# Grouping tokens by batch in the loads of an attention, soft mixture-of-experts and softplus kernel

## The chip, the cores and the metric

The kernel runs on one core of one Trainium2 chip. The metric is the device time of one execution in microseconds (us). An execution has five compute engines at its disposal (TensorE for matmuls and transposes, here PE; VectorE, DVE; ScalarE, ACT; GpSimd, POOL; SyncE, SP, which only issues DMAs here) and 16 DMA engines that move data between HBM and the on-chip memory of 128 partitions.

## What is computed

Three stages follow each other. q, k and v have the shape (8 batches, 8 heads, 576 tokens, 64). Attention is inside chunks of 64 tokens; the output is laid out as x with 8 x 576 = 4608 rows (tokens) of 512. A soft mixture of experts mixes all 4608 rows into 32 slots by a softmax over the tokens, runs 8 experts on their slots, and mixes the slots back into each token. A softplus layer ends it.

```python
def _attn_ref(q, k, v):                       # (8, 8, 576, 64) each
    chunk = 64; nc = S // chunk; scale = 1.0 / np.sqrt(D)
    scores = scale * np.matmul(q_c, k_c.transpose(0, 1, 2, 4, 3))   # per chunk
    attn = softmax(scores)
    out = np.matmul(attn, v_c)
x = attn_out.transpose(0, 2, 1, 3).reshape(B * S, H * D)            # (4608, 512)
logits = x @ phi                              # 32 slots
d = softmax of logits over the tokens
slot_out = per expert: relu((d.T @ x) @ w1[e]) @ w2[e]
x = (softmax of logits over the slots) @ slot_out
h = x @ w_in
g = np.maximum(h, 0.0) + np.log1p(np.exp(-np.abs(h)))
out = g @ w_out                               # (4608, 512)
```

## The kernel before

**Groups, pairs, units.** The 4608 tokens are cut into NG = 9 groups of GT = 512 in running order, over the ends of the batches: since a batch has 576 tokens, group 0 is the first 512 tokens of batch 0, group 1 the last 64 of batch 0 and the first 448 of batch 1, and so on, until group 8 is the last 512 tokens of batch 7. Each group has eight heads; a unit is two heads of a group (36 units), a pair is two units, four heads (18 pairs). Loads are by pair, work is by unit.

**Loads.** `load_q` (L297) loads q or k of a pair into a tile of 128 partitions; a partition holds four consecutive tokens of each head, 1 KB a head. `load_v` (L305) loads v in four blocks of 128 tokens, one token a partition, 256 bytes a head. Both ask `runs` (L288) for the stretches that lie in one batch and issue one DMA for each. So groups 0 and 8 load q in one piece of 128 partitions, and the others in two, of 16 and 112, 32 and 96, 48 and 80, 64 and 64, 80 and 48, 96 and 32, 112 and 16 partitions. In odd groups one block of v is split into 64 and 64. All DMAs are issued from SP, in order. q and k have two buffers each, v has three. Every issue also waits for the completion of the eighth DMA before it.

**The front.** For a unit: PE transposes q and k (`st_A`, L428), ACT copies them out (`st_B`, L440), PE makes the scores (`st_S`, L453), DVE subtracts the row maximum (L465, the one instruction of that line per unit, and L471), ACT takes the exponential, PE transposes (L486), PE multiplies with v (L505), DVE divides (L528), PE transposes the result x (L540). After the four units of a group come the logits (L556) and the running sums over tokens (up to `acc`, L624). Beside this, SP loads w_in in 16 pieces of 512 KB (`load_wi`, L340), which DVE, ACT and POOL convert, and some pieces of w1 (`load`, L326 and L329) that are parked until they are used.

**What sets the order.** `issue` is a list planner: it gives every step a rank and a cost by the table COST (SP: 3.4 for a load of q and k, 2.7 for v, 1.35 for w_in), and records the steps engine by engine in the order in which it would start them. The costs are those of the steps, not of the DMAs inside them.

**After the front.** The weights of the experts stream in through slots that are refilled as PE frees them (`emit_H`, `emit_SO`); their order is a list written by hand. The softplus stage then runs over 18 output tiles t of TT = 256 tokens, two per group, each in two halves i of 128 tokens (`emit_oc`, L1149, stores them). Inside a 512-token group, the odd tile has its two 64-token halves swapped over the partitions, so it is stored in two pieces of 64 rows.

Of the kernel before, what the change touches and what calls it, by code (L numbers as in the profile page):

```python
# [183 lines left out]
def kernel(  # L184
# [12 lines left out]
    nc = tc.nc  # L197
    B, H, S, D = q.shape
# [6 lines left out]
    TT = 256  # L205
    GT = 512
# [4 lines left out]
    NG = NT // GT  # L211
# [73 lines left out]
    vb = [ap.tile([128, 4, 4, VW], F32, name=f"vb{i}") for i in range(NV)]  # L285


    def runs(t0, n):  # L288
        done = 0
        while done < n:  # L290
            b, s = divmod(t0 + done, S)
            step = min(n - done, S - s)
            yield done, step, b, s
            done += step


    def load_q(src, t, pr, hs=range(4)):  # L297
        G, h0 = pr // 2, 4 * (pr % 2)
        for off, n, b, s in runs(G * GT, GT):
            nc.sync.dma_start(  # L300
                out=t[off // 4:(off + n) // 4, hs[0]:hs[-1] + 1],
                in_=src[b, h0 + hs[0]:h0 + hs[-1] + 1, s:s + n, :].rearrange(
                    "h (p r) d -> p h r d", r=4))

    def load_v(t, pr):  # L305
        G, h0 = pr // 2, 4 * (pr % 2)
        for m in range(4):
            for off, n, b, s in runs(G * GT + 128 * m, 128):
                nc.sync.dma_start(
                    out=t[off:off + n, m, :, 0:D],  # L310
                    in_=v[b, h0:h0 + 4, s:s + n, :].rearrange("h p d -> p h d"))

    def load(nm, n, sl):

# [89 lines left out]
    def st_l(pr):  # L404
        def f(e, held):
            ts = [rp_.tile([128, 4, 4, D], F32, tag=f"{nm}{held[nm, pr]}", name=nm)
                  for nm in "qk"]
            V["qk", pr] = ts
            for hs in (range(4),) if pr else (range(2), range(2, 4)):
                for src, t in zip((q, k), ts):  # L410
                    load_q(src, t, pr, hs)
        return f

    def st_lv(pr):
        def f(e, held):
            V["v", pr] = vb[held["v", pr]]
            load_v(V["v", pr], pr)
        return f
# [243 lines left out]
    for u in range(NU):  # L662
        G, hp = divmod(u, HP)
# [39 lines left out]
    for i in range(16):  # L703
        r = 2.0 * i + 3
# [21 lines left out]
    for i, (c, nms_, sls) in enumerate(ends):  # L726
# [4 lines left out]
        for sl in sls:  # L731
            n = next(n for n in home_of if home_of[n] == sl)
# [23 lines left out]
    for a in range(4):  # L756
# [4 lines left out]
        out=phi, in_=moe_phi.rearrange("(k p) s -> p k s", p=128)), rank=2.5)  # L761
# [9 lines left out]
        out=nM[:, 0], in_=nmr.rearrange("p g s -> p s g"), axis=AX.X, op=ALU.min)  # L771
# [10 lines left out]
        out=rep4w, in0=rep4[:, 0, :], scalar1=wc, scalar2=None, op0=ALU.mult)  # L782
# [22 lines left out]
    for kt in range(KD):  # L805
        nc.tensor.matmul(
            out=sp[:, kt, :], lhsT=acc.rearrange("p (c k) -> p k c", k=KD)[:, kt], rhs=rep4w,
# [124 lines left out]
    def ts_tile():  # L932
        return K["keep"].tile([128, 512], F32, tag="ts", name="ts", bufs=2)
# [215 lines left out]
    def emit_oc(n, i):  # L1149
        t = order[n][0]  # L1150
        po = V["po", t][i]
        if n in part_end:
            nc.scalar.copy(out=hold[2 * t + i], in_=po)
            return
        o = ts_tile()
        if t < NSP:
            nc.vector.tensor_tensor(out=o, in0=po, in1=hold[2 * t + i], op=ALU.add)
        else:
            nc.scalar.copy(out=o, in_=po)
        r0 = t * TT + i * 128  # L1160
        if t % 2 == 0:
            nc.sync.dma_start(out=out[r0:r0 + 128, :], in_=o)
        else:
            nc.sync.dma_start(out=out[r0:r0 + 64, :], in_=o[64:128, :])
            nc.sync.dma_start(out=out[r0 + 64:r0 + 128, :], in_=o[0:64, :])

    fns = {"za": emit_za, "z": emit_z, "zb": emit_zb, "H": emit_H, "open": emit_open,
           "c1": emit_c1, "c2": emit_c2, "c3": emit_c3, "c4": emit_c4, "c5": emit_c5,
# [11 lines left out]
    done = {x[1:] for x in MID if x[0] == "oc"}  # L1180
    for n in range(NQ + LAG + 1):
        for nm, d in seq:
            if last[nm] < n - d < NQ:
                fns[nm](n - d)
            m = n - LAG - 1
            if nm == "sp" and m >= 0 and (m in part_end or m in sum_end):
                for i in range(2):
                    if (m, i) not in done:
                        emit_oc(m, i)
# [30 lines left out]
```

## Time and profile before

| | |
|---|---|
| Timed runs, median of 3 | 724.42 us (723.98 to 725.68) |
| The profiled execution, its own time | 726.26 us |
| Its span in the profile | 724.5 us |
| PE, DVE, ACT, POOL busy | 655.6, 415.3, 344.9, 337.6 us |
| Loads and stores | 89.06 MB in 75072 packets |

The span is what the profile covers from the first to the last instruction; the execution's own time lies 1.76 us above it. A busy time is the sum of an engine's instructions. The DMA share is the sum of packet times over 16 engines, divided by the stretch: it can pass 1 where packets overlap in an engine. A packet is one contiguous run: 1 KB for q and k, 256 bytes for v, 4 KB for w_in, 8 KB for the 1 MB pieces of w1.

### The profile page before, as it was taken

Reading aid. Unit: us, or ns where it says so; the run is one execution under the profiler, and the core shown is the slowest. Engines: PE = TensorE matmul, PEld = TensorE weight load, DVE = VectorE, ACT = ScalarE, POOL = GpSimd, SP = SyncE. Lnnn points to the kernel's source line nnn. Section 1 sums busy time; section 2 is a strip of 40 time slices with the busy share of each in tenths; the row PEclk is TensorE's granted clock in tenths of the full one; section 3 lists DMA queues with packets and bytes.
Section 4 is the critical chain, followed back from the end, with each engine's and each line's share of the span. In section 5 each row is a group of like instructions: output and inputs, shape, how many; then the busy total and the mean of one; then the engine's idle time right before and its main releaser. Section 6 shows DMA issues by size and latency. Waiting matters only on the chain.

```text
span 724.5 us, 14077 instructions
## 1 busy us (share of the span) xinstructions
PE 655.6 (90%) x5811; PEld 518.7 (72%) x5811; DVE 415.3 (57%) x598; ACT 344.9 (48%) x525; POOL 337.6 (47%) x227
## 2 busy tenths in 40 slices
PE   7779867877779788999999999999999999999997
PEld 5657655766544454777778888888888888888886
DVE  2768767867649568798785544444444444444430
ACT  5779768868512324564545333333333333333340
POOL 4646657546213333868755444434443433333340
PEclk9999999989879999999999999999999999999999
DMA  9999999999969993000002111000010010100101
GB/s 241 224 220 256 214 245 237 254 243 263 392 254 379 414 410 134 1 1 0 1 0 59 37 51 30 30 9 21 30 30 29 1 30 29 30 1 29 30 30 29
DMA packets 75072, 89.06 MB, mean 123 GB/s; under 512 B 41856, under 2 KB 60288, under 8 KB 72832
## 3 DMA queue, kind: packets, MB, share of 16 engines
q1 hardware_dynamic: 75008, 88.16, 43.3%
q8 instruction: 46, 0.75, 0.5%
q14 instruction: 18, 0.15, 0.1%
HBM read 78.71 MB, written 9.44 MB: 122 GB/s over the span
## 4 chain that ended last, share of the span: by engine, by line
PE 65%; DVE 12%; DMA 11%; issue 5%; ACT 4%; POOL 3%; SPq 1%; ACTq 0%; POOLq 0%; DVEq 0%
PE trm L1144 15%; PE trm L1142 15%; PE trm L1146 15%; DMA k<-in_k_dram 7%; PE ph L1091 4%; PE tr L428 3%; PE hps L942 2%; PE X L505 2%; DMA g<-in_moe_w_dram 2%; ACT T L440 2%; PE S L453 2%; PE tr L540 2%; DMA w2a<-in_moe_w_out_dram 1%; DVE hTm L1104 1%; DVE cva L359 1%
## 5 line engine op out<-in xcount | busy, mean ns | idle before, releaser
L1125 POOL TENSOR_TENSOR g<-hTm,g 128x1024 fp32r<-128x1024 f32 (+1 forms) x48 | 112.7, 2347 | 143.9 <-ACT g L1121 143.9
L1110 ACT ACTIVATE hTm<-hTm 128x1024 f32<-128x1024 f32 (+2 forms) x51 | 51.5, 1010 | 160.2 <-DVE hTm L1104 160.2
L1104 DVE TENSOR_SCALAR hTm<-ph 128x1024 uint32<-128x1024 uint32 (+2 forms) x51 | 59.0, 1159 | 84.7 <-PE ph L1091 84.7
L440 ACT COPY T<-tr 64x512 f32<-64x512 f32 x144 | 90.2, 626 | 21.0 <-PE tr L428 19.0
L1125 POOL TENSOR_TENSOR g<-siT,g 128x1024 fp32r<-128x1024 f32 x24 | 58.1, 2419 | 62.4 <-ACT g L1121 62.4
L379 POOL TENSOR_TENSOR cvl<-cvl,cve 128x512 f32<-128x512 f32 x30 | 40.6, 1354 | 95.4 <-DVE cve L363 85.4
L1114 DVE SCALAR_TENSOR_TENSOR hTm<-ph,hTm 128x1024 f32<-128x1024 f32 (+2 forms) x51 | 59.1, 1159 | 39.6 <-ACT hTm L1110 39.6
L1110 ACT ACTIVATE siT<-siT 128x1024 f32<-128x1024 f32 x24 | 25.5, 1061 | 85.1 <-DVE siT L1104 85.1
L1091 PEld LDWEIGHTS ph<-cT,Tc 128*128 128x128 f32 x288 | 44.2, 191 | 16.7 <-issue 4.0
L1104 DVE TENSOR_SCALAR siT<-ph 128x1024 uint32<-128x1024 uint32 x24 | 29.3, 1222 | 43.0 <-PE ph L1091 43.0
L1091 PE MATMUL ph<-cT,Tc 128*128 128x256 f32 x288 | 48.1, 288 | 6.0 <-DVE hTm L1114 2.5
L1121 ACT CAST g<-hTm 128x1024 fp32r<-128x1024 f32 (+2 forms) x51 | 50.3, 989 | 2.2 <-DVE hTm L1114 2.2
L428 PE MATMUL tr<-ident,k 128*128 128x128 f32 x144 | 30.7, 298 | 13.0 <-DMA k<-in_k_dram 13.0
L1114 DVE SCALAR_TENSOR_TENSOR siT<-ph,siT 128x1024 f32<-128x1024 f32 x24 | 29.3, 1222 | 20.3 <-ACT siT L1110 20.3
L381 POOL TENSOR_TENSOR cvl<-cvl,cva 128x512 f32<-128x512 f32 x28 | 36.7, 1312 | 8.4 <-DVE cvl L379 6.5
L453 PE MATMUL S<-T 64*64 64x64 f32 x1152 | 28.9, 236 | 9.3 <-issue 4.5
L465 DVE TENSOR_REDUCE nm<-S 128x8 f32<-128x512 f32 x36 | 24.8, 688 | 21.3 <-PE S L453 20.8
L428 PE MATMUL tr<-ident,q 128*128 128x128 f32 x144 | 31.3, 302 | 6.1 <-DMA q<-in_q_dram 3.4
L547 DVE COPY xT<-tr 128x512 f32<-128x512 f32 x36 | 24.7, 686 | 17.2 <-PE tr L540 16.9
L453 PEld LDWEIGHTS S<-T 64*64 64x64 f32 x1152 | 23.9, 148 | 13.5 <-issue 7.2
L491 ACT COPY P<-tr 128x512 f32<-128x512 f32 x36 | 21.2, 588 | 22.4 <-PE tr L486 21.9
L540 PE MATMUL tr<-ident,x 128*128 128x128 f32 x144 | 24.9, 299 | 7.0 <-ACT T L440 3.3
(366 smaller groups left out, 1740.3 us busy)
## 6 DMA issues: line engine op xcount, KB each, us to landing
g<-in_moe_w_dram SPq DMA_DIRECT2D x12, 1024.0 KB, 10.2
vb<-in_v_dram SPq DMA_DIRECT2D x64, 128.0 KB, 7.1
d<-in_moe_w_dram SPq DMA_DIRECT2D x5, 1024.0 KB, 12.5
out_dram<-ts SPq DMA_DIRECT2D x18, 256.0 KB, 2.1
out_dram<-ts SPq DMA_DIRECT2D x36, 128.0 KB, 2.4
w0a<-in_moe_w_in_dram SPq DMA_DIRECT2D x8, 512.0 KB, 6.4
w0b<-in_moe_w_in_dram SPq DMA_DIRECT2D x8, 512.0 KB, 7.3
q<-in_q_dram SPq DMA_DIRECT2D x4, 448.0 KB, 6.5
```

Source lines behind the costliest of these rows:

```text
L428: nc.tensor.transpose(o[:, rr, :], t[:, 2 * (u % 2) + h, 2 * rr:2 * rr + 2, :].rearrange("p r d -> p (r d)"), ident)
L440: on(e)(out=t[64 * h:64 * h + 64, :, r2, :], in_=p[64 * r2:64 * r2 + 64])
L453: nc.tensor.matmul(out=sp[64 * o:64 * o + 64, b, 64 * i:64 * i + 64], lhsT=qT[64 * h:64 * h + 64, cs], rhs=kT[64 * h:64 * h + 64, cs], sta ...
L1091: nc.tensor.matmul(out=ph(n, a, b)[:, j - a, :], lhsT=K["Tc"][:, f * 128:(f + 1) * 128], rhs=K["cT"][:, t * TT:(t + 1) * TT], start=True, ...
L1104: nc.vector.tensor_scalar(out=scratch(n, a, b).bitcast(U32), in0=ph(n, a, b).bitcast(U32), scalar1=0x80000000, scalar2=None, op0=ALU.bitwi ...
L1110: nc.scalar.activation(out=y, in_=y, func=AF.Softplus)
L1114: nc.vector.scalar_tensor_tensor(out=y, in0=ph(n, a, b), scalar=0.0, in1=y, op0=ALU.max, op1=ALU.add)
L1121: nc.scalar.copy(out=V["gs", n][:, 0, a:b], in_=scratch(n, a, b))
L1125: tt(eng)(out=s[:, 1, a:b], in0=scratch(n, a, b), in1=s[:, 0, a:b].bitcast(F32), op=ALU.subtract)
L1142: nc.tensor.matmul(out=po, lhsT=s[:, 0, j, ts_], rhs=wr[:, hs], start=(n in begin and j == 0), stop=False)
L1144: nc.tensor.matmul(out=po, lhsT=s[:, 0, j, ts_], rhs=wr[:, ls], start=False, stop=False)
L1146: nc.tensor.matmul(out=po, lhsT=s[:, 1, j, ts_], rhs=wr[:, hs], start=False, stop=(j == 3 and (n in part_end or n in sum_end)))
```

## The change

A group is now the first 512 tokens of one batch: groups 0 to 3 are of batches 0 to 3, groups 5 to 8 of batches 4 to 7. Group 4 (`MIXED`) takes tokens 512 to 575 of all eight batches. In the whole groups each load of q or k is one DMA of 128 partitions and each block of v one DMA. In group 4, q and k are loaded head by head, each DMA from eight places of the source, and v in halves of 64 partitions. The stores follow the same map of rows. `runs` is gone.

```diff
+    MIXED = NG // 2
+
+    def batch_of(G):
+        return G - (G > MIXED)
 
     def load_q(src, t, pr, hs=range(4)):
         G, h0 = pr // 2, 4 * (pr % 2)
-        for off, n, b, s in runs(G * GT, GT):
-            nc.sync.dma_start(
-                out=t[off // 4:(off + n) // 4, hs[0]:hs[-1] + 1],
-                in_=src[b, h0 + hs[0]:h0 + hs[-1] + 1, s:s + n, :].rearrange(
-                    "h (p r) d -> p h r d", r=4))
+        if G == MIXED:
+            for h in hs:
+                nc.sync.dma_start(
+                    out=t[:, h].rearrange("x r d -> x (r d)"),
+                    in_=src[:, h0 + h, GT:S, :].rearrange("b (p r) d -> b p (r d)", r=4))
+            return
+        nc.sync.dma_start(
+            out=t[:, hs[0]:hs[-1] + 1],
+            in_=src[batch_of(G), h0 + hs[0]:h0 + hs[-1] + 1, 0:GT, :].rearrange(
+                "h (p r) d -> p h r d", r=4))
 
     def load_v(t, pr):
         G, h0 = pr // 2, 4 * (pr % 2)
         for m in range(4):
-            for off, n, b, s in runs(G * GT + 128 * m, 128):
-                nc.sync.dma_start(
-                    out=t[off:off + n, m, :, 0:D],
-                    in_=v[b, h0:h0 + 4, s:s + n, :].rearrange("h p d -> p h d"))
+            if G == MIXED:
+                for i in range(2):
+                    nc.sync.dma_start(
+                        out=t[64 * i:64 * i + 64, m, :, 0:D],
+                        in_=v[2 * m + i, h0:h0 + 4, GT:S, :].rearrange("h p d -> p h d"))
+                continue
+            nc.sync.dma_start(
+                out=t[:, m, :, 0:D],
+                in_=v[batch_of(G), h0:h0 + 4, 128 * m:128 * m + 128, :].rearrange(
+                    "h p d -> p h d"))
...
-        r0 = t * TT + i * 128
-        if t % 2 == 0:
-            nc.sync.dma_start(out=out[r0:r0 + 128, :], in_=o)
+
+        G, m = t // 2, 2 * (t % 2) + i
+        if G == MIXED:
+            rows = [(2 * m + j) * S + GT for j in range(2)]
         else:
-            nc.sync.dma_start(out=out[r0:r0 + 64, :], in_=o[64:128, :])
-            nc.sync.dma_start(out=out[r0 + 64:r0 + 128, :], in_=o[0:64, :])
+            rows = [batch_of(G) * S + 128 * m + 64 * j for j in range(2)]
+        if t % 2 == 0 and G != MIXED:
+            nc.sync.dma_start(out=out[rows[0]:rows[0] + 128, :], in_=o)
+            return
+        for j, r in enumerate(rows):
+            p0 = 64 * (j ^ t % 2)
+            nc.sync.dma_start(out=out[r:r + 64, :], in_=o[p0:p0 + 64, :])
```

The orders of PE, ACT, DVE and POOL are the same before and after, instruction for instruction. The order of SP differs inside the load steps only. On SP in group 1 (pairs 2 and 3), where `q`, `k` and `vb` are the tiles of q, k and v and `w0a`, `w0b` pieces of w_in, there stood before:

```order
L300 DMA q<-in_q_dram 16x4x256
L300 DMA q<-in_q_dram 112x4x256
L300 DMA k<-in_k_dram 16x4x256
L300 DMA k<-in_k_dram 112x4x256
L340 DMA w0b<-in_moe_w_in_dram 128x1024
L309 DMA vb_112<-in_v_dram 64x4x64 x2
L309 DMA vb_112<-in_v_dram 128x4x64 x3
```

and after the change:

```order
L303 DMA q<-in_q_dram 128x4x256
L303 DMA k<-in_k_dram 128x4x256
L349 DMA w0b<-in_moe_w_in_dram 128x1024
L317 DMA vb_112<-in_v_dram 128x4x64 x4
```

Nothing has moved past anything else: nine issues became seven, for the same bytes. On SP in group 4 (pair 8) there stood before:

```order
L300 DMA q<-in_q_dram 64x4x256 x2
L300 DMA k<-in_k_dram 64x4x256 x2
L309 DMA vb_112<-in_v_dram 128x4x64 x4
L340 DMA w0b<-in_moe_w_in_dram 128x1024
```

and after the change:

```order
L299 DMA q<-in_q_dram 128x1x256 x4
L299 DMA k<-in_k_dram 128x1x256 x4
L313 DMA vb_112<-in_v_dram 64x4x64 x8
L349 DMA w0b<-in_moe_w_in_dram 128x1024
```

Here nine issues became 17, again in the same place and for the same bytes.

## Rows read from the trace of the kernel before

**Rows 1.** The page: span, busy time of PE, and two lines of the 40 slices.
```profile
span 724.5 us, 14077 instructions
PE 655.6 (90%) x5811; PEld 518.7 (72%) x5811; DVE 415.3 (57%) x598; ACT 344.9 (48%) x525; POOL 337.6 (47%) x227
...
PE   7779867877779788999999999999999999999997
...
DMA  9999999999969993000002111000010010100101
```

**Rows 2.** Busy time by stretch: the front, the weight stage, the softplus stage.
```profile
core 0: us, PE busy (x) PEld busy (x) DVE busy (x) ACT busy (x) POOL busy (x), PEclk, DMA share, GB/s
0.00:208.90 208.90, 160.53 (x3264) 125.98 (x3265) 142.81 (x313) 147.27 (x275) 109.03 (x113) 0.92 1.05 261
208.90:280.00 71.10, 61.19 (x524) 34.05 (x525) 47.54 (x86) 21.67 (x41) 24.41 (x19) 0.86 0.88 348
280.00:724.50 444.50, 433.85 (x2025) 358.63 (x2023) 224.94 (x200) 176.00 (x210) 204.14 (x96) 1.00 0.08 22
```

**Rows 3.** Timeline of DVE: row maximum of units 4, 16, 20 and 32 (start, us, ...).
```profile
28.24 0.69 DVE L465 TENSOR_REDUCE nm<-S 128x8 f32<-128x512 f32 x1
...
90.38 0.69 DVE L465 TENSOR_REDUCE nm<-S 128x8 f32<-128x512 f32 x1
...
113.50 0.69 DVE L465 TENSOR_REDUCE nm<-S 128x8 f32<-128x512 f32 x1 [0.40 <-PE S L453]
...
177.23 0.69 DVE L465 TENSOR_REDUCE nm<-S 128x8 f32<-128x512 f32 x1 [0.82 <-PE S L453]
```

**Rows 4.** Timeline of SP's queue: q of pairs 5 to 7; parked w1.
```profile
40.71 3.29 SPq L300 DMA_DIRECT2D q<-in_q_dram  x2
...
50.18 3.14 SPq L300 DMA_DIRECT2D q<-in_q_dram  x2
...
60.26 3.15 SPq L300 DMA_DIRECT2D q<-in_q_dram  x2
...
64.46 0.46 SPq L329 DMA_DIRECT2D g<-in_moe_w_dram  x1
...
91.16 0.42 SPq L326 DMA_DIRECT2D w1a<-in_moe_w_dram  x1
...
157.72 0.42 SPq L329 DMA_DIRECT2D g<-in_moe_w_dram  x1
```

**Rows 5.** DMA view of 2 to 12, of 140 to 158, of 158 to 176 us.
```profile
DMA packets 4304, 2.87 MB, mean 287 GB/s; under 512 B 2208, under 2 KB 4239, under 8 KB 4304
...
q1 hardware_dynamic: 4304, 2.87, 98.3%
...
DMA packets 6244, 4.16 MB, mean 231 GB/s; under 512 B 3998, under 2 KB 6046, under 8 KB 6174
...
q1 hardware_dynamic: 6242, 4.13, 114.1%
...
DMA packets 6151, 5.11 MB, mean 284 GB/s; under 512 B 3730, under 2 KB 5765, under 8 KB 6021
```

**Rows 6.** Busy time from 57 to 79 us, columns as in rows 2.
```profile
57.00:79.00 22.00, 19.23 (x462) 15.14 (x464) 19.87 (x44) 19.56 (x36) 14.66 (x12) 1.00 1.04 246
```

**Rows 7.** PE's waits from 13 to 158 us (total, times, longest); landing of k's loads.
```profile
PE tr L428 <- DMA k<-in_k_dram: 12.6, 8, 3.3
...
PE tr L428 <- DMA q<-in_q_dram: 2.0, 2, 1.1
...
DMA to landing us min/median/max: 2.9/7.0/9.4
```

**Rows 8.** The page's DMA issues: stores (count, KB each, us to landing).
```profile
out_dram<-ts SPq DMA_DIRECT2D x18, 256.0 KB, 2.1
out_dram<-ts SPq DMA_DIRECT2D x36, 128.0 KB, 2.4
```

More of the change, by code (lines that the diff above doesn't have):

```diff
@@ L285 @@
     vb = [ap.tile([128, 4, 4, VW], F32, name=f"vb{i}") for i in range(NV)]
[L288 to L294, printed above, removed]
+    MIXED = NG // 2
+    def batch_of(G):
+        return G - (G > MIXED)
     def load_q(src, t, pr, hs=range(4)):
         G, h0 = pr // 2, 4 * (pr % 2)
-        for off, n, b, s in runs(G * GT, GT):
-            nc.sync.dma_start(
-                out=t[off // 4:(off + n) // 4, hs[0]:hs[-1] + 1],
-                in_=src[b, h0 + hs[0]:h0 + hs[-1] + 1, s:s + n, :].rearrange(
-                    "h (p r) d -> p h r d", r=4))
+        if G == MIXED:
[8 more added lines that the diff above has]
+                "h (p r) d -> p h r d", r=4))
     def load_v(t, pr):
```

## The prediction

> **What bounds the kernel now.** I read the page first [rows 1]: PE is busy 90% of the span, so the end of the kernel, where PE never rests, cannot be moved by a load. But the DMA line is at 9 in 14 of the first 15 of 40 slices and near 0 soon after, and PE is at 7 or 8 in most of those. The table by stretch then cuts the span in three [rows 2]: the attention front to 208.9 us, the weight stage to 280 us, and the softplus stage of 444.5 us, in which the DMA engines are busy 8% and PE 433.85 us. Only the front loads q, k and v, so only it is touched. In it no compute engine is full (PE 160.53, ACT 147.27, DVE 142.81 of 208.9 us), and the DMA share is 1.05: the loads are the fullest resource.
>
> How fast the front goes I read from the row-maximum instruction on DVE, one per unit (a unit is two heads of a group; 36 in all, 18 pairs) [rows 3]. The first unit of group 1 stands at 28.24 us, that of group 8 at 177.23: 149.0 us for 14 pairs, 10.64 us each. Group 4 alone (90.38 to 113.50) took 23.1 us, so the other six groups between took 125.9 us for 12 pairs, 10.49 us each.
>
> Now the loads themselves. A pair brings q and k (512 KB each), v (four of 128 KB) and mostly one 512 KB piece of w_in: 2.10 MB. In the queue's own order the loads stand back to back: q and k of three pairs in a row begin at 40.71, 50.18 and 60.26 us [rows 4], near 10 us a pair, as the compute does. And two stretches that move packets of the same mean size differ [rows 5]: from 2 to 12 us, when all loads are whole (128 partitions: group 0, with w_in and phi), 4304 packets with 2.87 MB are 667 bytes each and go at 287 GB/s with a share of 0.983, so a packet holds an engine 0.983 x 16 x 10 us / 4304 = 36.5 ns; from 140 to 158 us, when group 7 comes in pieces of 112 and 16 partitions, 6242 packets of 666 bytes go at 231 GB/s, 1.141 x 16 x 18 us / 6242 = 52.6 ns each, 1.44 times as long. Group 8 is whole again: from 158 to 176 us the rate is 284 GB/s [rows 5]. The split groups 1 to 7 are the slow ones; that is what the change aims at.
>
> **The change part by part.**
> 1. Loads of groups 1, 2, 3, 5, 6, 7 become whole. The orders of PE, ACT, DVE and POOL do not change at all; on SP the two pieces of q and of k become one each, and a v block that lay in two batches becomes one. Bytes and packets stay the same. A pair's 2.10 MB take 9.1 us at 231 GB/s and 7.3 us at 287. Beside that 14 pairs carry some 5.2 MB of w1 parked early (four of 1 MB and one of 2 x 512 KB; the first, the one in halves and the last stand in [rows 4]), 0.375 MB a pair: 2.47 MB in all, 10.7 us at 231 GB/s, which is the measured pace, and 8.6 us at 287. So the loads would allow 8.6 us a pair.
> 2. What the compute then allows. In 57 to 79 us the front ran at its best for 22 us [rows 6]: DVE made 44 of its instructions, at 313 / 18 = 17.4 a pair 2.53 pairs or 8.7 us each; ACT 36 at 275 / 18 = 15.3 a pair, 2.36 pairs or 9.3 us each; DVE was busy 90%. I take 9.0 us a pair. The bounds: below, 8.6 (loads) with ACT's bare work at 147.27 / 18 = 8.2; above, 10.49 as now. Six groups at 9.0 take 108.0 us in place of 125.9: 17.9 us gained. What is late next is ACT and DVE, and PE behind them.
>    From the side of the waits [rows 7]: between 13 and 158 us PE stood 12.6 us for k and 2.0 for q. These 14.6 us are what PE itself shows; that ACT, DVE and PE's issue idle behind late loads is not in it, so 17.9 is more than it but of its size.
> 3. Group 4 becomes the mixed group, the last 64 tokens of every batch. Its q and k come in four pieces of 128 KB each in place of two of 256 KB, its v in eight halves of 64 partitions in place of four whole blocks: for its two pairs 16 pieces of q and k, 16 of v, with two of w_in and two halves of w1, 36 in all. The trace has no such load. Eight pieces at most are under way, since each issue also waits for the completion of the eighth before it: 4.5 rounds. At the shortest landing of a k load, 2.9 us, they take 13.1 us, less than the compute's 18.0; at the median, 7.0 us, 31.5 us [rows 7]. So the group takes 18.0 to 31.5 us. The median is a landing behind a full queue of pieces up to 512 KB, and these are smaller, but there are more of them; I take a value between, the 23.1 us of today, no gain and no loss. The loads of q and k run up to two pairs ahead, which covers part of what is late; at the high end 8.4 us are lost.
> 4. The first 28 us and the last 31.7 us (177.23 to 208.9) hold whole loads already: nothing. Group 1's first unit waited for a split piece, worth a us perhaps; it goes into the range.
> 5. Stores: tile 8 of the output, even, is stored in four halves in place of two wholes: two stores more, 2.4 us to landing against 2.1 [rows 8]. They lie in the softplus stage with DMA at 8% [rows 2], and only the tile that they leave, one of two buffers, waits for them: nothing.
> 6. The weight stage starts when the front ends, and its w1 and w2 loads follow the slots that its matmuls free. It moves as a whole and keeps its 71 us; so does the last stage. The gain of the front reaches the end undiminished.
>
> Sum: 17.9 us off the profiled execution's 726.26 us (span 724.5) gives 708.4; that run is 1.84 us above the median of the timed runs, 724.42, so the forecast for the median is 724.42 - 17.9 = **706.5 us**.
>
> **The rivals.**
> - **The mixed group is served by half of the engines.** Its q and k are read batch by batch, eight batches outermost in the source, and a transfer dealt out by that dimension would use eight of sixteen. q and k of a pair, 1.05 MB, take 3.65 us at 287 GB/s, 7.3 at half, and with the 1.44 of partition crowding 10.5 us; the rest of the pair 3.65: 14.2 a pair, 28.4 for the group, 5.3 more than taken: 711.8 us. For it: the shape of the source. Against: no row of the trace shows a transfer on few engines, and the run-ahead hides some. [...]
> - **Compute follows wherever the loads lead.** 12 pairs at 8.6 are 103.2, the mixed group 2 x 8.6 = 17.2: 120.4 against 149.0, 28.6 gained: 695.8 us. For it: PE's granted clock in the front is 0.92 on average against 1.00 in the good stretch of 57 to 79 us [rows 2, 6], so fewer gaps may also speed PE. Against: ACT and DVE at 89 to 90% there.
> - **Waits change their name.** Only half of PE's 14.6 us comes back, the rest goes to ACT, DVE and code fetch: 717.1 us. Against: the rows 3 pace agrees with the load rate to a tenth of a us.
> - **Nothing happens**, because the slow packets come from mixing v, w_in and w1 and not from the pieces: 724.4 us. Against: 158 to 176 us has the same mix, w1 too, at 284 GB/s.
> - **Slower.** The mixed group's pieces stall the pipe by both mechanisms at once: the two rounds of q and k count double because half of the engines serve them, 6.5 rounds in all, each at the median landing of 7.0 us: 45.5 us, 22.4 more than now, less 17.9 gained elsewhere: 728.9 us. It decides from a group time of 23.1 + 17.9 = 41.0 us upward, a round of 6.3 us. Against: the 7.0 us include a queue that the change empties, and eight of these pieces are 1 MB at most, where eight of today's loads are up to 3 MB.
>
> **How the numbers follow.** Forecast 706.5 (0.55); half the engines 711.8 (0.16); compute follows 695.8 (0.12); waits change name 717.1 (0.10); nothing 724.4 (0.03); slower (0.04). The range, 696 to 717 us, takes in the second, third and fourth cases' times and leaves out the slow and void cases and the far sides: about 2 in 10. Faster by over 0.2% (1.4 us, about what a measurement of this kernel can tell from no change): 0.93; within: 0.03; slower: 0.04.
>
> **What would show it.** In the profile after: the row-maximum pace between groups 1 and 8 at 131 us in place of 149.0, near 18 us for each whole group; packets of 667 bytes near 37 ns and the rate in the front up while the share falls to 1.0 or less; PE's waits for k and q well under 14.6 us; the same 515.6 us from the front's end to the end. Wrong: a group 4 over 28 us (half the engines, or rounds), a pace of 10 with a DMA share below 0.9 (compute bound all along), or split and whole packets alike.

## The result, and the profile after

The changed kernel takes 712.18 us (median of four runs, 710.35 to 715.69), the kernel before beside it 724.20 (721.97 to 725.68): a ratio of 0.9836, with a 95% interval of 0.9801 to 0.9870. The forecast was 706.5 us in a range of 696 to 717. So it is faster, inside the range, by two thirds of what was forecast: 12.0 us in place of 17.9. A few executions of two kernels further below (the ones of whole and of last mixed loads) were disturbed; their ratios leave those out.

The profiled execution took 711.07 us. From its page, the span, PE's busy time and the 40 slices of PE and DMA:

```profile
span 709.3 us, 14058 instructions
PE 652.4 (92%) x5811; PEld 515.8 (73%) x5811; DVE 415.9 (59%) x598; ACT 344.9 (49%) x525; POOL 337.7 (48%) x227
...
PE   7899768888799688998999999999999999999997
...
DMA  9988699999979970000002110010110010100101
```

Against [rows 1] the span is 15.2 us shorter and the busy times are the same to 3.2 us: what went is idle time. PE's line has more of 8 and 9 in the front than it had. The fifth and sixth slice (71 to 106 us) stand out, with PE at 7 and 6, and with DMA at 6 in the first of them.

The same three stretches as in [rows 2], the front cut 1.4 us after the start of the last running sum on DVE, as it was there (stretch, its length, busy us and instructions of each engine, granted clock of PE, DMA share, GB/s):

```profile
core 0: us, PE busy (x) PEld busy (x) DVE busy (x) ACT busy (x) POOL busy (x), PEclk, DMA share, GB/s
0.00:193.00 193.00, 157.01 (x3265) 123.31 (x3265) 143.21 (x313) 147.10 (x275) 109.16 (x113) 0.91 0.93 277
193.00:264.30 71.30, 61.49 (x522) 33.81 (x523) 46.98 (x85) 21.88 (x41) 24.36 (x19) 0.86 0.91 364
264.30:709.30 445.00, 433.91 (x2027) 358.69 (x2025) 225.67 (x201) 175.90 (x210) 204.18 (x96) 1.00 0.08 22
```

The front is 15.9 us shorter, the weight stage and the softplus stage keep their length (71.3 and 445.0 against 71.10 and 444.50 us): all that happened, happened in the front. There the loads run at 277 GB/s in place of 261, with a share of 0.93 in place of 1.05.

Where in the front, the row-maximum rows on DVE tell, units 4, 16, 20 and 32 as in [rows 3] (start, us, engine, line, operation), and under them the last running sum:

```profile
29.36 0.69 DVE L474 TENSOR_REDUCE nm<-S 128x8 f32<-128x512 f32 x1
...
79.65 0.64 DVE L474 TENSOR_REDUCE nm<-S 128x8 f32<-128x512 f32 x1
...
108.59 0.69 DVE L474 TENSOR_REDUCE nm<-S 128x8 f32<-128x512 f32 x1 [0.40 <-PE S L462]
...
165.26 0.69 DVE L474 TENSOR_REDUCE nm<-S 128x8 f32<-128x512 f32 x1 [0.82 <-PE S L462]
...
191.60 0.75 DVE L633 SCALAR_TENSOR_TENSOR acc<-acc,al,tr 128x512 f32<-128x512 f32 x1 [2.54 <-PE tr L623]
```

From unit 4 to 32 it is 135.9 us in place of 149.0. Group 4 takes 28.9 of them (79.65 to 108.59) in place of 23.1, so the six whole groups take 107.0 in place of 125.9. The account of the 15.2 us, in order of time: the first unit of group 1 comes 1.1 us later (29.36 against 28.24); six whole groups, 18.9 us less; group 4, 5.8 us more; from unit 32 to the front's end 27.7 us in place of 31.7, 4.0 less; the rest of the kernel 0.8 more (516.3 us against 515.6). The sum is 15.2, to the rounding. The two larger terms that were not foreseen are group 4 and the end of the front.

**The whole groups.** First the stretch of [rows 6] again, then groups 1 to 3 (29.4 to 79.6 us) and groups 5 to 7 (108.6 to 165.3 us). Under them stands the view of the DMA engines from 140 to 158 us, when group 7 came in pieces before [rows 5]:

```profile
57.00:79.00 22.00, 20.64 (x490) 15.86 (x494) 21.12 (x48) 20.99 (x42) 14.67 (x12) 1.00 0.75 219
29.40:79.60 50.20, 45.34 (x1065) 35.44 (x1057) 46.13 (x102) 47.97 (x89) 34.69 (x28) 1.00 0.82 234
108.60:165.30 56.70, 48.24 (x1102) 38.40 (x1105) 47.90 (x107) 50.08 (x96) 37.90 (x30) 0.97 0.97 276
```

```profile
DMA packets 6687, 5.04 MB, mean 280 GB/s; under 512 B 4315, under 2 KB 6361, under 8 KB 6556
...
q1 hardware_dynamic: 6684, 4.99, 97.7%
```

DVE is busy 96% and ACT 95% of 57 to 79 us. The DMA share of 0.75 beside that is not the share of whole loads, since from 62.81 us on SP issues those of the mixed pairs (below). The longer stretches show two paces. Groups 1 to 3 take 50.3 us, 8.4 a pair, with ACT busy 96% and DVE 92%: there the compute sets the pace. Groups 5 to 7 take 56.7 us, 9.4 a pair, with ACT at 88% and DVE at 84%, and there the DMA engines are all but full again (a share of 0.97 at 276 GB/s, 2.6 MB a pair; 0.93 in e10): four of the five megabytes of parked w1 are issued behind the mixed pairs. e5 below, in which every group loads whole, has the same two paces, 8.4 us a pair in groups 1 to 3 and 9.4 in groups 4 to 7, with a share of 1.03 at 288 GB/s from 98.8 to 155.4 us.

In the DMA view the mix of packets is not that of before, so the engine time is best told for each megabyte: 0.977 x 16 engines x 18 us / 4.99 MB = 56.4 us of an engine a megabyte. By [rows 5] it was 54.8 from 2 to 12 us, with whole loads, and 79.6 from 140 to 158 us, with split ones. What SP's queue waited for from 28 to 160 us (total, times, longest) has the matmul that frees a buffer of v at its head. Of these 20.9 us 19.7 lie behind 108 us, so in groups 5 to 7 the loads wait for the compute too, and no run separates which of the two holds the pace there:

```profile
SPq L317 <- PE X L514: 20.9, 9, 5.3
```

**The mixed group.** PE's waits from 13 to 158 us, and under them where they stand in PE's timeline (in brackets the idle time before, and what ended it). The last row is the stretch behind the longest wait (columns as above, the granted clock third from the end):

```profile
PE tr L437 <- DMA q<-in_q_dram: 5.2, 2, 4.3
PE tr L437 <- DMA k<-in_k_dram: 3.5, 2, 2.8
```

```profile
79.74 0.38 PE L437 MATMUL tr<-ident,k 128*128 128x128 f32 x2
81.04 0.41 PE L437 MATMUL tr<-ident,q 128*128 128x128 f32 x2 [0.92 <-DMA q<-in_q_dram]
84.22 0.69 PE L437 MATMUL tr<-ident,k 128*128 128x128 f32 x2 [2.77 <-DMA k<-in_k_dram]
...
98.65 0.69 PE L437 MATMUL tr<-ident,q 128*128 128x128 f32 x2 [4.28 <-DMA q<-in_q_dram]
100.02 0.69 PE L437 MATMUL tr<-ident,k 128*128 128x128 f32 x2 [0.68 <-DMA k<-in_k_dram]
```

```profile
98.60:101.20 2.60, 1.87 (x8) 1.43 (x8) 0.00 (x0) 0.46 (x1) 0.00 (x0) 0.50 1.11 228
```

In [rows 7] PE waited 14.6 us for q and k, spread over ten places; now it waits 8.7 us, and all of it in group 4: 3.7 us for its own second pair (pair 9), and 5.0 for pair 10, which is a whole pair again. Less these 8.7 us the group would stand at 20.2. The same transpose is longer behind such a stop: 0.38 us at 79.74, at a granted clock of 1.00 (from 79.70 to 82.50 us), and 0.69 behind the longer waits, where the granted clock is 0.50 (from 84.20 to 85.30 us, and in the last row).

SP's queue at that place (start, how long the issues took together, line, tile, count):

```profile
62.81 4.84 SPq L299 DMA_DIRECT2D q<-in_q_dram  x4
67.75 2.52 SPq L299 DMA_DIRECT2D k<-in_k_dram  x4
70.37 5.85 SPq L313 DMA_DIRECT2D vb<-in_v_dram  x8
76.39 0.48 SPq L349 DMA_DIRECT2D w0b<-in_moe_w_in_dram  x1
76.96 2.60 SPq L299 DMA_DIRECT2D q<-in_q_dram  x4
79.65 2.52 SPq L299 DMA_DIRECT2D k<-in_k_dram  x4
82.26 5.43 SPq L313 DMA_DIRECT2D vb<-in_v_dram  x8
87.86 0.48 SPq L349 DMA_DIRECT2D w0a<-in_moe_w_in_dram  x1
88.39 0.42 SPq L335 DMA_DIRECT2D w1a<-in_moe_w_dram  x1
88.86 0.43 SPq L335 DMA_DIRECT2D w1b<-in_moe_w_dram  x1
89.39 1.40 SPq L303 DMA_DIRECT2D q<-in_q_dram  x1
```

SP goes from one issue to the next without a gap (what an issue waits is in its time). The 36 issues of the two mixed pairs, with two pieces of w_in and two of w1 among them, hold it from 62.81 to 89.39, 26.6 us, where two pairs of the whole groups take 17 to 19 us. In 5.6 of the 26.6 us SP itself waits for PE to free a buffer, so this is not the price of issuing alone. Pair 10 is the one that pays: its q is issued behind the last of them and behind two 512 KB halves of w1, and lands 9.3 us later (98.65).

### The profile page after: what moved, and what is told of

It reads as the page before. It is cut to its first block, busy times and chain, and to the rows that moved or that the text cites. A ratio compares the mean times of both kernels' runs of the same rounds, so it can differ in the third digit from the quotient of the medians.

```text
span 709.3 us, 14058 instructions
## 1 busy us (share of the span) xinstructions
PE 652.4 (92%) x5811; PEld 515.8 (73%) x5811; DVE 415.9 (59%) x598; ACT 344.9 (49%) x525; POOL 337.7 (48%) x227
## 4 chain that ended last, share of the span: by engine, by line
PE 68%; DVE 13%; ACT 9%; issue 4%; DMA 4%; POOL 2%; SPq 0%; ACTq 0%; DVEq 0%; POOLq 0%
PE trm L1153 16%; PE trm L1151 15%; PE trm L1155 15%; ACT T L449 5%; PE ph L1100 4%; DMA k<-in_k_dram 3%; PE hps L951 2%; PE tr L437 2%; PE S L462 2%; PE X L514 2%; PE tr L549 2%; PE sops L992 2%; DVE cva L365 1%; PE tr L495 1%; DVE cvl L393 1%
## 5 line engine op out<-in xcount | busy, mean ns | idle before, releaser
L1119 ACT ACTIVATE siT<-siT 128x1024 f32<-128x1024 f32 x24 | 25.5, 1061 | 84.8 <-DVE siT L1113 84.8
L1130 ACT CAST g<-hTm 128x1024 fp32r<-128x1024 f32 (+2 forms) x51 | 50.3, 989 | 2.2 <-DVE hTm L1123 2.2
L474 DVE TENSOR_REDUCE nm<-S 128x8 f32<-128x512 f32 x36 | 24.6, 685 | 15.9 <-PE S L462 15.4
L556 DVE COPY xT<-tr 128x512 f32<-128x512 f32 x36 | 24.6, 683 | 15.2 <-PE tr L549 14.9
L514 PE MATMUL X<-vb,P 64*64 64x65 f32 x1152 | 27.9, 233 | 3.3 <-issue 2.4
## 6 DMA issues: line engine op xcount, KB each, us to landing
vb<-in_v_dram SPq DMA_DIRECT2D x64, 128.0 KB
out_dram<-ts SPq DMA_DIRECT2D x40, 128.0 KB
```

Source lines behind the costliest of these rows:

```text
L1119: nc.scalar.activation(out=y, in_=y, func=AF.Softplus)
L1130: nc.scalar.copy(out=V["gs", n][:, 0, a:b], in_=scratch(n, a, b))
```

## The experiments

All kernels below are the changed kernel with one edit. "Six groups" and "group 4" are read from the row-maximum rows as above; "end" is from unit 32 to the start of the last running sum. The ratios are to the kernel before, run beside each.

| kernel | ratio (95% interval) | six groups | group 4 | end |
|---|---|---|---|---|
| before | 1 | 125.9 | 23.1 | 30.3 |
| after | 0.9836 (0.9801 to 0.9870) | 107.0 | 28.9 | 26.3 |
| e10, after once more | 0.9823 (0.9785 to 0.9862) | 107.9 | 30.5 | 30.2 |
| e1, halves of 64 partitions | 1.0070 (1.0043 to 1.0098) | 128.0 | 32.3 | 27.2 |
| e2, halves by heads | 0.9791 (0.9741 to 0.9841) | 105.9 | 30.7 | 26.4 |
| e3, mixed q and k whole | 0.9729 (0.9680 to 0.9778) | 106.7 | 25.6 | 25.5 |
| e4, 16 outermost in the source | 0.9815 (0.9771 to 0.9860) | 108.3 | 28.3 | 28.7 |
| e5, mixed group all whole | 0.9688 (0.9578 to 0.9798) | 106.9 | 18.8 | 30.2 |
| e6, whole groups in 16 pieces | 1.0253 (1.0183 to 1.0323) | 138.3 | 28.2 | 26.3 |
| e7, true costs | 0.9755 (0.9694 to 0.9816) | 108.3 | 20.4 | 28.7 |
| e11, e7 once more | 0.9751 (0.9720 to 0.9781) | 108.3 | 19.7 | 27.0 |
| e8, mixed last | 0.9722 (0.9653 to 0.9792) | | | |
| e9, w1 halves later | 0.9838 (0.9810 to 0.9867) | 111.2 | 25.2 | 28.4 |
| e12, mixed last, true costs | 0.9735 (0.9705 to 0.9766) | 111.3 | 20.4 | 25.4 |

### Was it the partitions, or the number of pieces? (e1, e2)

The two kernels load q and k of each whole group between 1 and 7 in two DMAs of 256 KB each. In e1 each fills 64 partitions; in e2 each fills all 128, with two of the four heads. The number of issues, of bytes and of packets is the same.

```diff
+        if G not in (0, NG - 1):
+            for i in range(2):
+                nc.sync.dma_start(
+                    out=t[64 * i:64 * i + 64, hs[0]:hs[-1] + 1],
+                    in_=src[batch_of(G), h0 + hs[0]:h0 + hs[-1] + 1,
+                            256 * i:256 * i + 256, :].rearrange("h (p r) d -> p h r d", r=4))
+            return
```

> The changed kernel, but q and k of the whole groups 1, 2, 3, 5, 6, 7 come again in two pieces, of partitions 0 to 63 and 64 to 127, from one batch. Theory A (crowding: a piece on part of the partitions is written by all sixteen engines at once, and that makes its packets and those beside it longer): packets of about 667 bytes go back from near 37 to near 52 ns, the six groups from 107.0 us back to about 125, the time from 712 to about 730 us. Rival B (the number of issues on the queue): as slow as the run with two pieces by heads, both near 730. Rival C (the crossing of a batch, that is where in HBM the pieces lie): no change, 712, since each piece lies in one batch.

```diff
+        if G not in (0, NG - 1):
+            for i in range(0, 4, 2):
+                nc.sync.dma_start(
+                    out=t[:, i:i + 2],
+                    in_=src[batch_of(G), h0 + i:h0 + i + 2, 0:GT, :].rearrange(
+                        "h (p r) d -> p h r d", r=4))
+            return
```

> The changed kernel, but q and k of the whole groups 1, 2, 3, 5, 6, 7 come in two pieces by heads (two heads each, all 128 partitions): the same bytes, packets and number of issues as with two pieces by partitions. Theory A (crowding on part of the partitions): like the changed kernel, 712 us, packets near 37 ns. Rival B (number of issues): like the pieces by partitions, near 730 us. Rival C: 712.

e1 takes 730.89 us and gives back all of the gain, e2 takes 712.21 and loses nothing. The engine time from 140 to 158 us, first of e1 and then of e2:

```profile
DMA packets 5327, 3.69 MB, mean 205 GB/s; under 512 B 3976, under 2 KB 5069, under 8 KB 5197
...
q1 hardware_dynamic: 5325, 3.65, 100.3%
```

```profile
DMA packets 6769, 5.28 MB, mean 293 GB/s; under 512 B 4336, under 2 KB 6384, under 8 KB 6638
...
q1 hardware_dynamic: 6766, 5.23, 100.0%
```

That is 79.1 us of an engine a megabyte in e1 (1.003 x 16 x 18 / 3.65) and 55.1 in e2, against 79.6 with the split loads of before and 54.8 with whole ones [rows 5]. So the engines are equally busy and move 1.44 times less when each load of q and k fills only half of the partitions. The factor is that of this stretch: from 28 to 160 us it is 70.0 us a megabyte in e1 and 56.0 in e2, 1.25 times. By size, the trace's packet records from 140 to 158 us have a median of 81 ns for the 1 KB packets of q and k in e1 and 76 before, and 46 in e2 and after. The 256-byte packets of v take 27 ns in e1, where v's loads are whole, and 18 in e2: the short loads go with slower packets of the whole ones beside them. PE's waits for q and k from 13 to 158 us in e1 follow:

```profile
PE tr L444 <- DMA k<-in_k_dram: 17.4, 8, 3.7
PE tr L444 <- DMA q<-in_q_dram: 12.2, 4, 5.3
```

29.6 us, twice the 14.6 of before. Partitions that a load leaves out are shown to be the cause of the slow packets (79.1 against 55.1 us a megabyte), and the number of pieces is shown not to be; by what mechanism, no row shows. The cuts of before (112 and 16 partitions, for one) were as slow (79.6) as 64 and 64, but were not varied by themselves.

### What makes the mixed group long? (e3, e5, e4)

In e3 group 4 loads q and k like a whole group (its branch in `load_q` is switched off), in e5 v too. It then gets the first 512 tokens of batch 4, so the last 64 tokens of each batch are left out.

```diff
-        if G == MIXED:
+        if G < 0:
```

> The changed kernel, but the mixed group loads q and k like a whole group, the first 512 tokens of batch 4, so its scores are of other tokens; v stays in halves. It shows what the mixed q and k cost. Theory H (half of the engines serve them): the mixed group (row maximum of unit 16 to that of unit 20) falls from 28.9 to about 20 us, the time from 712 to about 703 us; the DMA share there rises from 0.6 to about 0.9. Rival V (the eight halves of v and the w1 pieces behind them hold the queue): 26 us or more, time within 3 us of 712.

> The changed kernel, but the mixed group loads q, k and v like a whole group, the first 512 tokens of batch 4, so its attention is of other tokens. It shows what the mixed group's loads cost in all. Theory I (the many issues on SP, 17 a pair, and the half of the engines hold the group): unit 16 to unit 20 falls from 28.9 us to 18 to 20, the time to about 702 us. Rival W (the two w1 halves parked behind this group and the order planned hold it, not its loads): the group stays at 24 us or more, about 707 us, as with whole q and k alone.

Group 4 goes from 28.9 to 25.6 us in e3 and to 18.8 in e5, where it is a group like the others; in e5 0.8 us is all that PE waits for q and k between 13 and 158 us. So with the order as it is planned the loads of the mixed group make the whole of its excess. Taken out after q and k, the v halves of 64 partitions, eight a pair, are the larger part of it (6.8 us against 3.3); whether by their number or by the partitions that they leave out, no run separates. e5's front is 6.0 us shorter at the last running sum (185.6 against 191.6), though its end is 3.9 longer; its ratio is the least certain of the table.

The rival of the prediction was that q and k of the mixed group, with eight batches outermost in the source, are served by half of the engines. e4 takes the tokens outermost, 16 of them, in the same number of DMAs; the order of the tokens inside the tile is then undone where PE's transposes write.

```diff
-                    in_=src[:, h0 + h, GT:S, :].rearrange("b (p r) d -> b p (r d)", r=4))
+                    in_=src[:, h0 + h, GT:S, :].rearrange("b (p r) d -> p b (r d)", r=4))
...
+                if u // HP == MIXED:
+                    o = p[:, i].rearrange("x (b p rr) -> x rr p b", b=B, rr=2)
```

> The changed kernel, but in the mixed group the partitions run token block by token block with the batch inside, so that the source's outermost dimension is 16 long instead of 8; the transposes write their columns back in batch order. Still 16 pieces of q and k of 128 KB. Theory H (the outermost dimension of 8 holds a load to eight engines): q and k of the mixed group now run on sixteen, the group falls from 28.9 to about 21 us, the time to about 704 us. Rival P (many small pieces, eight under way at most): the group stays at 28 us or more, 712 us. Should the neighbouring partitions of an engine crowd as in theory A, packets of 1 KB there are half as long again and about half of the gain is left: 708 us.

The DMA share from 62 to 76 us in 40 slices, in tenths, first of after and then of e4:

```profile
DMA  9989999999866544554434445557688756656536
```

```profile
DMA  9898999996210575887589524667854461716362
```

In after the engines are mostly 4 to 5 tenths busy from 66.5 to 71 us (a share of 0.49 of that stretch), when hardly anything but q and k of pair 8 is under way; in e4 they are mostly at 5 to 9 behind a gap. So the share does look like half of the engines, and the other order of the source does raise it. But group 4 takes 28.3 us in place of 28.9, and the time is 713.20: hardly anything hung on it. The transposes that undo the order are no longer than after's (0.38 us), so they do not hide a gain. The share fits the rival, but half of the engines is not what makes the group long; how many engines serve a load, no row tells.

### What do many small issues cost? (e6)

e6 loads the whole groups between 1 and 7 in as many pieces as the mixed one, but each on all 128 partitions: q and k head by head, v in halves of two heads.

```diff
+            for i in range(hs[0], hs[-1] + 1):
+                nc.sync.dma_start(
+                    out=t[:, i].rearrange("x r d -> x (r d)"),
+                    in_=src[batch_of(G), h0 + i, 0:GT, :].rearrange("(p r) d -> p (r d)", r=4))
...
+                for i in range(0, 4, 2):
+                    nc.sync.dma_start(
+                        out=t[:, m, i:i + 2, 0:D],
+                        in_=v[batch_of(G), h0 + i:h0 + i + 2, 128 * m:128 * m + 128, :].rearrange(
+                            "h p d -> p h d"))
```

> The changed kernel, but the whole groups 1, 2, 3, 5, 6, 7 load q and k in four pieces each (one head, 128 partitions) and v in eight (two heads, 128 partitions): 17 issues a pair as in the mixed group, all on sixteen engines and all partitions. It tells the price of the issues alone. Theory I (an issue of such a piece occupies SP for 0.6 to 0.7 us, so 17 take 10 to 12 us a pair): the six groups rise from 107 us toward 130, the time to about 735 us. Rival H (half of the engines is what holds the mixed group, issues are free): 712 us.

It takes 741.37 us, the slowest kernel here. Busy times from 28 to 160 us (columns as above), the engine time from 140 to 158 us, and the issues of q (count, ns shortest/median/longest, first and last start):

```profile
28.00:160.00 132.00, 96.66 (x2031) 76.96 (x2029) 87.68 (x194) 91.68 (x170) 71.10 (x55) 0.90 0.75 212
```

```profile
q1 hardware_dynamic: 4601, 4.19, 77.6%
```

```profile
L305 SPq DMA_DIRECT2D q<-in_q_dram x48: 376/428/1524, 13.7 to 166.6; - x48
L299 SPq DMA_DIRECT2D q<-in_q_dram x8: 596/606/795, 79.4 to 93.5; - x8
```

The packets are quick (0.776 x 16 x 18 / 4.19 = 53.3 us of an engine a megabyte), the DMA engines are only 75% busy, no compute engine is full, and yet six groups take 138.3 us against 107.0: 31.3 us for 12 pairs, 2.6 a pair. PE waits 23.9 us for q and k between 13 and 158 us. Here nothing is crowded; the loads are simply too many. How much of it is SP's time for an issue (0.43 us in the median, 0.61 for the pieces of the mixed group) and how much the wait of each issue for the eighth before it, the run does not separate. The planner, too, still counts these loads as whole ones, which e7 below shows to matter; e6 with true costs was not run, so a part of the 2.6 us may be the order's.

### Where the lateness goes: the planner's costs (e7, e11, e9)

The planner counts 3.4 us of SP for q and k of a pair and 2.7 for v, in the mixed group too, where they took 7.4 and 5.9, then 5.1 and 5.4 (the rows of SP above). e7 tells it 6.5 and 5.6, and changes no load:

```diff
+        if nm in ("lq", "lv") and key // 2 == MIXED:
+            s.cost = {"SP": 6.5 if nm == "lq" else 5.6}
```

> The changed kernel, but the planner is told what the mixed group's loads take of SP: 6.5 for q and k of a pair and 5.6 for v, in place of 3.4 and 2.7. The loads themselves are as in the changed kernel; only the order of the steps around them moves. If part of the 28.9 us of the group is the order (w1 halves issued between the mixed pairs and the next q and k): 25 us and 708. If it is the loads alone: 712 within 2 us.

> The changed kernel with the planner's true costs of the mixed loads again, beside the changed kernel: 706 us, 0.976 of the kernel before, if the gain seen is the order's and not the chip's; 712 if not.

e7 takes 705.99 us and, run again beside after, e11 takes 706.20 against 711.36 for e10. The intervals of the ratios of e11 and e10 do not meet, so these 5.2 us are real. From 60 to 115 us (columns as above), first after, then e11:

```profile
60.00:115.00 55.00, 42.14 (x874) 33.15 (x874) 39.01 (x85) 41.34 (x77) 32.32 (x25) 0.88 0.84 247
```

```profile
60.00:115.00 55.00, 45.59 (x1043) 35.38 (x1043) 49.83 (x105) 47.54 (x89) 38.72 (x30) 1.00 0.85 218
```

In the same 55 us DVE makes 105 instructions in place of 85, ACT 89 in place of 77, and PE keeps the full granted clock (1.00 in place of 0.88), with a DMA share that has hardly changed (0.85 against 0.84). The mixed loads themselves are no quicker: SP is at them from 61.04 to 88.90 us, 27.9 us against 26.6.

```profile
61.04 4.07 SPq L299 DMA_DIRECT2D q<-in_q_dram  x4
...
88.90 0.56 SPq L303 DMA_DIRECT2D q<-in_q_dram  x1
...
95.42 1.93 SPq L303 DMA_DIRECT2D q<-in_q_dram  x1
...
103.20 1.88 SPq L303 DMA_DIRECT2D q<-in_q_dram  x1
...
110.37 2.22 SPq L303 DMA_DIRECT2D q<-in_q_dram  x1
```

What differs is the work around them. On SP the pieces of w1 that stood behind pair 9 and between the pairs after it have moved towards the end of the front, so pairs 10 to 13 begin 7.2 us apart (88.90 to 110.37) where after has 9.5 (89.39, 99.11, 106.47, 117.83). On PE the first transposes of pair 9 come later (84.66 us in place of 81.04) and find their loads landed, and those of pair 10, whose q is issued no earlier than in after, begin at 96.01 in place of 98.65. e11 has no wait for q or k between 13 and 158 us. So a sum of issues that is longer than the compute beside it is not by itself a wait. A part of the lateness does move: group 3 takes 18.4 us in e11 and 16.4 in after.

e9 asks which of the two it is. It moves only the parked pieces of w1 but the first behind pair 10, on SP; PE, ACT, DVE and POOL keep after's order.

```diff
-        add("lw", n, at(load, "w1", n, home_of[n]), rank=100 + n)
+        add("lw", n, at(load, "w1", n, home_of[n]), [("lv", 10)] if n else (),
+            rank=100 + n)
```

> The changed kernel, but the two parked w1 halves (512 KB each) that stand between the mixed group's loads and q and k of the next pair are issued a pair and a half later; the orders of PE, ACT, DVE and POOL do not change. Theory W (1 MB of parked weights in front of the next q and k is what makes the mixed group's lateness show): unit 16 to 20 falls from 28.9 to about 26 us (1.05 MB at 380 GB/s is 2.8 us), the time from 712 to about 709. Theory M (the many issues of the mixed group alone; PE's order planned on too low a cost): 28 us or more, 712.

Group 4 falls to 25.2 us, and the wait for pair 10's q is gone (1.1 us for its k is left). But PE's waits from 75 to 105 us are still there for the rest:

```profile
PE tr L437 <- DMA k<-in_k_dram: 3.8, 2, 2.7
PE tr L437 <- DMA q<-in_q_dram: 3.1, 1, 3.1
```

and groups 5 to 7, which now carry the w1 pieces, take 21.0, 20.9 and 20.0 us where after has 20.2, 18.3 and 18.2: 5.2 us more. Its time, 713.01 us, is that of e10, 711.36, by the intervals. So the two halves of w1 were where the lateness was paid, not what caused it: moved by one pair, they are paid for one group later. What e11 has beside that is the order of the compute engines and the far move of w1; which of these two brings the rest was not tried.

### The mixed group at the end (e8, e12), and after again (e10)

In e8 the mixed group is group 8, in e12 with the costs of e7 as well.

```diff
-    MIXED = NG // 2
+    MIXED = NG - 1
```

> The changed kernel, but the mixed group is the ninth, not the fifth. Theory I: the same 17 issues a pair and half of the engines cost the same 9 to 12 us, now at the end of the front, where units 32 to 35 stretch from 13 to over 20 us and the parked w1 loads behind them come later too: 712 to 718 us. Rival W (what costs is the w1 halves beside the mixed loads): the middle groups go at 17 to 18 us each and the end stretches less than 5 us: 706 us.

> The mixed group as the ninth, and the planner told its true costs. If the mixed group's price is the order around its loads, the last place has no next pair behind it to be late and the time is 702 us or less, below both kernels and below the fifth place with true costs (706). If it is the loads themselves, 706 to 712.

> The changed kernel again, on the same chip as its variants: 712 us, 0.984 of the kernel before.

e8 has a ratio of 0.9722 (0.9653 to 0.9792) and, at 703.67 us, lies below both of its expectations; e12 has one of 0.9735 at 706.35 us. With e11 (0.9751) they are one result by their intervals: about 18 to 20 us below the kernel before and 5 to 8 below after. True costs and another place for the odd group both work, and do not add up. e12 missed the 702 us that its expectation gave for an order that is the whole price, and fell where it had put the loads themselves. e12's group 4, now whole, takes 20.4 us and its end, with the mixed loads, 25.4, no more than elsewhere. But its seven whole groups take 131.7 us where those of e5 take 125.8; why was not looked into. e10 confirms the long mixed group: 30.5 us, with 9.2 us of PE's waits for q and k in it. It also shows how far the account of one profile can be trusted, since its end takes 30.2 us where after's took 26.3.

## Why the prediction held, and where it was off

1. **Whole loads (first step): right.** The step took packets of split loads to be 1.44 times longer because of the partitions they leave out, and predicted 287 GB/s for whole ones. e1 and e2 show the cause, with 79.1 against 55.1 us of an engine a megabyte. The prediction's own sign, packets of 667 bytes near 37 ns, could not be read as put, since the mix of packets changed; by megabyte it is 56.4 against 54.8, and a 1 KB packet fell from 76 to 46 ns.
2. **9.0 us a pair (second step): the sum right, its reason for one half.** Six whole groups take 107.0 us, 107.9 in e10; 108.0 was forecast. But 9.0 is the mean of two paces, and that it came out so is in part luck. Groups 1 to 3 go at 8.4 us a pair, below the 8.6 that the step had as the floor of the loads, with ACT busy 96% and DVE 92%: there the compute holds them, as the step said. Groups 5 to 7 go at 9.4 with the DMA engines 97% busy and ACT 88%. The first step spread the parked w1 evenly over the pairs, and most of it comes behind the mixed ones. "Compute follows wherever the loads lead" (8.6 a pair, 695.8 us) held in the first half and not in the second, not even in e5 without a mixed group.
3. **The mixed group (third step): the term that was mis-sized.** The step took 23.1 us, between bounds of 18.0 and 31.5; it is 28.9 and 30.5. The choice in the middle had no row behind it. It counted rounds of eight landings and let the run-ahead hide a part. What the runs show in its place is waits of PE, 8.7 of the 28.9 us: 3.7 for pair 9, whose transposes come before its loads have landed, and 5.0 for pair 10, whose loads stand behind all the issues of the mixed pairs and two pieces of w1. That a planner built on the costs of whole loads would place PE's transposes too early was not considered at all, though the costs stand in the code: with true costs the same loads, which keep SP as long (27.9 us), make a group of 19.7 to 20.4 us. What the number of the pieces (2.6 us a pair in e6, with the old costs) and the half-filled partitions of v would each cost under a right order stays open.
4. **The first 28 us and the end of the front (fourth step):** the start came 1.1 us later instead of equal. The end was 4.0 us shorter in the profiled execution and 0.1 in e10's; over the profiles of the table it lies between 25.4 and 30.3 us. From 165.3 to 191.6 us after's loads run at 393 GB/s with a share of 1.01, but PE's recorded waits there are for other engines and none is for a load, so what makes this stretch vary stays open. It may also be why the profile's gain (15.2 us) is above that of the medians (12.0): e10's profile has 8.6.
5. **Stores, weight stage, softplus stage (steps five and six): right**, 516.3 us against 515.6.

**The rivals.** "Half of the engines" gave 711.8 us, the nearest of all the times, and its sign, a group over 28 us, appeared. No row shows its eight engines; what one shows is the share of 0.49 from 66.5 to 71 us. e4 refutes it as the cause: the order that takes the half share away wins 0.6 us, so its nearness is luck. "Waits change their name" (717.1) is refuted by the pace of the whole groups. "Slower" needed a mixed group of 41.0 us; by e1 (730.89 us) the slow packets, and by e6 (741.37 us) the many pieces, can each bring the whole kernel over 724 us, but there the whole groups have them too. The range of 696 to 717 us was said to take in the times of three rivals; 695.8 and 717.1 lie just outside it.

## What to carry to other kernels

Let each load fill all partitions, and cut it by another dimension where it must be cut: two DMAs of 128 partitions (256 KB each) cost what one does here (712.21 against 712.18 us), and with two of 64 the whole mix of loads cost 1.25 to 1.44 times the engine time (70.0 against 56.0 and 79.1 against 55.1 us a megabyte). Where such a change leaves one odd piece of work, look at what is issued ahead of its data and at when an engine that works in order first asks for them: the same loads made a wait of 8.7 us in one order and none in another. And when the cost of a load changes, the table that orders the work around it must be told: that was worth 5 us here, and moved no byte.

## What was not expected of the hardware

The issue of a load on SP itself has a price by shape: medians of 0.43 us for one head of q on 128 partitions in e6, and 0.61 for a head of the mixed group out of eight batches, with the same bytes. And the DMA engines can be 75% busy with quick packets while PE waits 23.9 us for q and k (e6): a share under 1 does not mean that loads have room.
